# Transposes and values one step nearer to the scores, in an attention that runs into a mixture of experts

## The chip, the cores and the metric

One core of a Trainium2 chip runs the whole program. The metric is the device time of one launch in microseconds. A core has five engines with a queue of instructions each: TensorE (PE, with its weight loads shown as PEld), VectorE (DVE), ScalarE (ACT), GpSimd (POOL) and SyncE (SP), which here issues nearly all the loads and stores.

## The reference

q, k and v have 4 batches, 8 heads, 576 positions and 64 columns a head. Half of the heads see the last 32 positions, the other half every 32nd position back; the rest is masked away.

```python
scores = np.where(masks, scale * (q @ k.T), -1e9)
attn = np.exp(scores - max); attn /= attn.sum(-1) + 1e-9
x = (attn @ v) as [2304, 512]
P = exp(x @ w_gate - max); 8 rounds of row and column normalization
out = sum over 8 experts e of P[:, e:e+1] * (np.maximum(x @ w1[e], 0) @ w2[e])
```

## The kernel before

The attention is cut into 32 steps: 4 batches, 4 pairs of heads, 2 halves of the positions. A step has 4 to 6 blocks of 64 keys. Its parts are functions of their own:

- `load_qk` and `load_v` issue its loads on SP; a tile of q and k has 3 buffers, one of v has 5.
- `at_scores` (line 251) makes the scores on PE in 20 to 40 small matmuls, into both PSUM buffers of the tag "s".
- `at_masks` (270) scales, masks and finds the extremes on DVE, block by block; `at_exp` (281) takes the exponentials on ACT. For the steps in `early` ACT leaves the sums out.
- `at_normalize` makes 1e-9 plus the sum and its reciprocal on DVE (291, 292; before them the sum itself, line 290, for the steps in `early`), and POOL multiplies (293).
- `at_transpose` transposes the result on PE (303), and DVE copies it out of PSUM (307, 309).
- `at_values` multiplies by v on PE (329). `x_high` (ACT, 361) and `x_low` (DVE, 366) write the result into x as two parts, a rounded one and the rest. Every product of the experts is made of three products of such parts.

Work is put into each engine's queue in the order of the code, and an engine takes its queue in order. There are first 8 rounds (`at_k` 0 to 7, loop at line 1123), which hold almost only attention. They also split the first weight tiles of expert 0: `split_w` rounds on ACT (193) and subtracts on POOL (194). `begin_layer1` (450) puts first products of expert 0 into late rounds, and `keep_busy` (1118) matmuls that nobody reads. Then come 36 slots (line 1214). A slot holds 12 matmuls of the first layer (`layer1`), their relu (467, 468), 6 matmuls of the second layer (`layer2`, line 487), and in the first 27 slots one step's share of the attention, each part of another step. In slots 6, 7, 13, 14, 20 and 21 the gate's products and transposes stand too (378, 387). From slot 4 on POOL prepares sums and weights for the later part (565, 581, 649 to 653, 194). After the slots come the other 7 experts, in which PE's products are made by a scheme with fewer multiplications, and the attention has no part.

In a slot the order is: layer 1, `attention_values` (values of step `at_k - 3`, x, loads), `attention_scores` (scores, masks, exponentials of step `at_k`), layer 2 of the slot before, `attention_rest` (transposes of step `at_k - 2`, then the normalizing of `at_k - 1`), and POOL's work at the end. Slot s has `at_k` = 8 + s.

Of the kernel before, what the change touches and what calls it, by code (L numbers as in the profile page):

```python
# [8 lines left out]
F32 = mybir.dt.float32  # L9
# [57 lines left out]
def kernel(  # L67
# [10 lines left out]
    P = 128  # L78
# [3 lines left out]
    NP = NDT  # L82
# [19 lines left out]
    pools = {}  # L102
# [39 lines left out]
    def chunk(ci):  # L142
        n = min(CH, NT - ci * CH)
        o = 2 * NDT * CH * ci
        return reg[:, o : o + 2 * NDT * n].rearrange("p (i k t) -> p i k t", i=2, k=NDT)
# [63 lines left out]
    NS = len(steps)  # L209
    QK = -(-max(sum(_columns(*x)[:2]) + BR for x in STEPS) // P) * P  # L210
    qk_t, v_t, scored, sms, sums_t, pts, moved, mxs = ({} for _ in range(8))

    def load_qk(k):
        if k < NS:
            nq, nk, _ = _columns(*steps[k][1:])
            t = pools["qkv"].tile([P, QK], F32, tag="qk", name=f"qk_{k}", bufs=3)
            blocks = _blocks(*steps[k][1:])
            q0, ks, m = blocks[-1]
            end = nq + max(nk, ks[-1] + BR)
            nc.sync.dma_start(t[:, :end], qkv[k, :, :end])  # L220
            qk_t[k] = t

    def load_v(k):
        if k < NS:
            nq, nk, nv = _columns(*steps[k][1:])
            blocks = _blocks(*steps[k][1:])
            n, nh = len(blocks), len(blocks[0][1])
            half = -(-n // 2) * nh * 2 * DH
            tv = pools["qkv"].tile([P, 6 * 2 * DH], F32, tag="v", name=f"v_{k}", bufs=5)
            src = qkv[k, :BR, nq + nk : nq + nk + nv]  # L230
            for i, v in enumerate((src[:, :half], src[:, half:])):
                nc.sync.dma_start(tv[BR * i : BR * (i + 1), : v.shape[1]], v)
            v_t[k] = tv[:, :half].rearrange("p (n h j d) -> p n h j d", h=nh, j=2, d=DH)

    def at_scores(k):
        b, p, hf = steps[k]
        t = qk_t.pop(k)
        nq = _columns(p, hf)[0]
        blocks = _blocks(p, hf)
        n = len(blocks)  # L240
        half = -(-n // 2)
        order = [i + half * x for i in range(half) for x in range(2) if i + half * x < n]
        scs = [ps.tile([P, 3, BR], F32, tag="s", name=f"sc_{k}_{i}") for i in range(2)]
        for i in order:
            q0, ks, _ = blocks[i]
            m, par = BR // len(ks), i // half
            for j in range(2):
                sl = slice(DH * j, DH * j + DH)
                for h, k0 in enumerate(ks):
                    o = BR * (j ^ par) + m * h  # L250
                    nc.tensor.matmul(  # L251
                        scs[par][o : o + m, i % half, :], t[sl, q0 + m * h : q0 + m * h + m],
                        t[sl, nq + k0 : nq + k0 + BR], start=True, stop=True,
                    )
        scored[k] = scs, order, half

    def at_masks(k):
        b, p, hf = steps[k]
        scs, order, half = scored.pop(k)
        n = len(order)  # L260
        sums_t[k] = st_p.tile([P, 6], F32, tag="sums", name=f"sums_{k}")
        sm = pools["at"].tile([P, 6, BR], F32, tag="sm", name=f"sm_{k}")
        mx = mxs[k] = st_p.tile([P, 6], F32, tag="mx", name=f"mx_{k}")
        for c, i in enumerate(order):
            if _is_local(p):
                mask = mlocal if hf or i else mlocal0
            else:
                mask = mstrided

            nc.vector.tensor_tensor_reduce(  # L270
                out=sm[:, c, :], in0=scs[i // half][:, i % half, :], in1=mask[:, :BR],
                op0=ALU.add, op1=ALU.min, scale=-SCALE, scalar=3.0e38,
                accum_out=mx[:, c : c + 1],
            )
        sms[k] = sm, n
# [10 lines left out]
    def at_normalize(k):  # L286
        sm, n = sms[k]
        rs = sums_t.pop(k)[:, :n]
        if k in early:
            nc.vector.tensor_reduce(rs, sm[:, :n, :], axis=AX.X, op=ALU.add)  # L290
        nc.vector.tensor_scalar_add(rs, rs, 1e-9)
        nc.vector.reciprocal(rs, rs)
        nc.gpsimd.tensor_tensor(
            sm[:, :n, :], sm[:, :n, :], rs.unsqueeze(2).to_broadcast([P, n, BR]), op=ALU.mult
        )

    def at_transpose(k):
        sm, n = sms.pop(k)
        pt = pts[k] = pools["qkv"].tile([P, 3, P], F32, tag="pt", name=f"pt_{k}", bufs=3)
        tp = ps.tile([P, 3, P], F32, tag="t", name=f"tp_{k}")  # L300
        for c in range(0, n, 2):
            m = min(2, n - c)
            nc.tensor.transpose(  # L303
                tp[: m * BR, c // 2, :],
                sm[:, c : c + m, :].rearrange("p n k -> p (n k)"), ident,
            )
        nc.vector.tensor_copy(pt[:, : n // 2, :], tp[:, : n // 2, :])
        if n % 2:
            nc.vector.tensor_copy(pt[:BR, n // 2, :], tp[:BR, n // 2, :])
# [49 lines left out]
    def x_high(k):  # L359
        for src, (hi, _) in moved[k]:  # L360
            nc.scalar.activation(hi, src, AF.Copy)

    def x_low(k):
        b = steps[k][0]
        for src, (hi, lo) in moved.pop(k):
            nc.vector.tensor_tensor(lo, src, hi.bitcast(F32), op=ALU.subtract)
        p, hf = steps[k][1:]
        if hf:
            done.extend(
                (c, p) for c in range(NC) if b * S < min(NT, (c + 1) * CH) <= (b + 1) * S  # L370
            )
# [167 lines left out]
    for p in range(NPASS):  # L539
        for k in range(NK):  # L540
            k = (k - KEEP * p) % NK
# [523 lines left out]
            next(w2n, None)  # L1065


    LAG = 3
    at_k = 0

    def attention_scores():
        if at_k < NS:
            at_scores(at_k)
            at_masks(at_k)
            at_exp(at_k)

    def attention_rest():


        nonlocal at_k  # L1080
        if 0 <= at_k - 2 < NS:
            at_transpose(at_k - 2)
        if 0 <= at_k - 1 < NS:
            at_normalize(at_k - 1)
        at_k += 1

    def attention_values():
        if at_k > WARM + 2:
            store_x(1)
        if at_k > WARM + 1:  # L1090
            at_values(at_k - LAG, "tt")
            x_high(at_k - LAG)
            x_low(at_k - LAG)
        load_qk(at_k + 2)
        load_v(at_k)

    WARM = 2 * NP - 1
    nc.scalar.dma_start(cst[:, 2:], consts[:, 2:])
    nc.scalar.dma_start(cst[:, 0], consts[:, 0])
    for k in range(3):  # L1100
        load_qk(k)
    load_v(0)
    for i in range(2):
        nc.sync.dma_start(cst[BR * i : BR * (i + 1), 1], consts[:BR, 1])
    spare = chunk(NC - 1)[:, 0, :, :].rearrange("p k t -> p (k t)")[:, : 5 * P]
    nc.gpsimd.memset(spare.bitcast(F32), 1.0)
    nc.gpsimd.memset(ones, 1.0)
    nc.gpsimd.memset(wgs.bitcast(F32), 0.0)
    for o in (QT, 3 * QT):
        nc.gpsimd.tensor_copy(cst[o : o + QT, 3, :BR], cst[o : o + QT, 2, :BR])  # L1110
    ahead = {5: [(0, (0, 1))], 6: [(1, (0, 1))], 7: [(0, (2,)), (1, (2,))]}
    early = {4: 0, 5: 1, 6: 2, 7: 3}
    late = {0: 4, 1: 5, 2: 6, 3: 7}

    def keep_busy(n, tag="l1"):
        unread = ps.tile([P, 4 * P], F32, tag=tag, name=f"unread_{at_k}_{n}")
        for _ in range(n):
            nc.tensor.matmul(unread, spare[:, :P], spare[:, P:], start=True, stop=True)  # L1118

    FILL = (1, 0, 1, 1, 0, 0, 1)  # L1120
    keep_busy(6)
    at_scores(0)
    for at_k in range(WARM + 1):
        last = at_k == WARM
        if at_k == 0:
            load_v(1)
        if at_k < WARM:
            load_qk(at_k + 3)
        if at_k not in (0, 2):
            load_v(max(2, at_k))  # L1130
        if at_k not in (0, 3):
            load_w()
        if at_k >= 3:
            x_high(at_k - 3)
        at_masks(at_k)
        if at_k:
            at_normalize(at_k - 1)
        if at_k >= 3:
            x_low(at_k - 3)
        if at_k >= 2:  # L1140
            at_transpose(at_k - 2)
        if at_k < 2:
            keep_busy(1)
        if at_k < WARM:
            at_scores(at_k + 1)
        at_exp(at_k)
        if last:
            begin_layer1(0, (0, 2 * P), *ahead[at_k][0])
        if at_k >= 2:
            at_values(at_k - 2, "yy")  # L1150
        for x in ahead.get(at_k, ())[last:]:
            begin_layer1(0, (0, 2 * P), *x)
        if at_k and FILL[at_k - 1]:
            keep_busy(FILL[at_k - 1], "l1" if at_k < 3 else "t")
        if last:
            x_high(at_k - 2)
            x_low(at_k - 2)
        if at_k in early:
            split_w(*plain[early[at_k]])
    at_k = WARM + 1  # L1160
# [231 lines left out]
```

## Time and profile before

| | us |
|---|---|
| median of 3 runs | 1535.34 (1533.87 to 1536.08) |
| the profiled execution | 1534.33 |
| its span from the first to the last instruction | 1532.5 |
| PE busy | 1521.8 |
| DVE busy | 1302.3 |
| POOL busy | 1041.0 |
| ACT busy | 546.3 |

The profiled execution lies 1.0 us below the median; 1.8 us of it lie outside the span. A busy PE is one with a matmul under way, whatever it waits for inside.

### The profile page before, as it was taken

The page shows a single profiled execution, that of the slowest core. Times are in us where ns is not written, and L with a number is a line of the kernel's source. Part 1 is how long each engine was busy: PE and PEld are TensorE (multiplying, and loading weights), DVE is VectorE, ACT ScalarE, POOL GpSimd, SP SyncE. Part 2 cuts the span into 40 slices and gives each one's busy share as a digit, 9 for nine tenths or more (in the row PEclk, how much of TensorE's full clock was granted, in tenths as well). Part 3 has the DMA queues.
Part 4 walks back from the last instruction along what each step waited for, and adds up shares of the span by engine and source line. Part 5 has one row for each costly group of instructions (what it writes and reads, how often), then busy time and mean ns, then how long its engine had stood idle before and what let it go on. Part 6 is the DMA issues. An engine that isn't in the chain of part 4 may idle for free.

```text
span 1532.5 us, 27898 instructions
## 1 busy us (share of the span) xinstructions
PE 1521.8 (99%) x10096; PEld 1445.4 (94%) x10096; DVE 1302.3 (85%) x2610; ACT 546.3 (36%) x1340; POOL 1041.0 (68%) x1056
## 2 busy tenths in 40 slices
PE   8999999999999999999999999999999999999999
PEld 6888989899999999899999999999999999999998
DVE  6665899999999999768888888888688888888888
ACT  7675344334343434242332322322323232232221
POOL 4567155555666565078888889888687787777874
PEclk9999999999999999999999999999999999999999
DMA  9778888988888888887877867767576676666662
GB/s 275 246 237 274 319 321 309 344 309 336 312 329 319 325 329 295 331 305 264 318 259 277 311 237 296 294 247 286 212 306 262 261 283 239 268 264 239 277 246 91
DMA packets 145625, 431.11 MB, mean 281 GB/s; under 512 B 35696, under 2 KB 89168, under 8 KB 130512
## 3 DMA queue, kind: packets, MB, share of 16 engines
q1 hardware_dynamic: 145200, 429.14, 75.4%
q8 instruction: 80, 1.31, 0.3%
q14 instruction: 57, 0.47, 0.1%
q10 hardware_dynamic: 288, 0.20, 0.0%
HBM read 284.54 MB, written 144.75 MB: 280 GB/s over the span
## 4 chain that ended last, share of the span: by engine, by line
PE 98%; DMA 1%; DVE 1%; ACT 0%; POOL 0%; issue 0%; SPq 0%; POOLq 0%; ACTq 0%
PE p L882 27%; PE bb L731 18%; PE yg L763 18%; PE bc L731 12%; PE ba L731 12%; PE y L487 3%; PE ph L450 3%; PE pv L329 1%; PE sc L251 1%; PE tp L303 1%; PE pl L378 1%; PE tr L912 0%; DMA qk<-in_qkv 0%; PE unread L1118 0%; ACT sm L281 0%
## 5 line engine op out<-in xcount | busy, mean ns | idle before, releaser
L890 DVE TENSOR_TENSOR total<-p,total 128x384 f32<-128x384 f32 x770 | 401.0, 556 | 0.8 <-PE p L882 0.8
L731 PE MATMUL bb<-reg 128*128 128x384 f32 x1620 | 325.9, 335 | 0.0
L731 PEld LDWEIGHTS bb<-reg 128*128 128x128 f32 x1620 | 284.9, 188 | 2.9 <-DVE u L805 0.3
L731 PE MATMUL bc<-reg 128*128 128x384 f32 x1080 | 216.2, 334 | 0.0
L731 PE MATMUL ba<-reg 128*128 128x384 f32 x1080 | 216.2, 334 | 0.0
L863 ACT ACTIVATE a<-u 128x384 fp32r<-128x384 f32 x114 | 59.9, 526 | 384.5 <-DVE u L857 382.8
L805 DVE TENSOR_TENSOR u<-bb,m 128x384 f32<-128x384 f32 x180 | 99.9, 555 | 111.4 <-PE bb L731 108.9
L731 PEld LDWEIGHTS bc<-reg 128*128 128x128 f32 x1080 | 190.1, 188 | 0.0
L731 PEld LDWEIGHTS ba<-reg 128*128 128x128 f32 x1080 | 189.8, 188 | 0.0
L939 POOL TENSOR_TENSOR s1t<-m,u 128x384 f32<-128x384 f32 x57 | 57.9, 1016 | 163.3 <-DVE m L857 163.3
L770 DVE SCALAR_TENSOR_TENSOR acc<-yg,gate,acc 128x512 f32<-128x512 f32 x197 | 139.1, 740 | 9.0 <-PE yg L763 9.0
L763 PE MATMUL yg<-w2t,h 128*128 128x512 f32 x540 | 125.5, 390 | 0.0
L763 PE MATMUL yg<-w2b,h 128*128 128x512 f32 x540 | 125.4, 390 | 0.0
L882 PE MATMUL p<-s,w2b 128*128 128x384 f32 x696 | 125.3, 334 | 0.0
L882 PEld LDWEIGHTS p<-s,w2b 128*128 128x128 f32 x696 | 121.1, 188 | 0.0
L882 PE MATMUL p<-s,w2t 128*128 128x384 f32 x672 | 121.0, 334 | 0.0
L763 PEld LDWEIGHTS yg<-w2t,h 128*128 128x128 f32 x540 | 101.1, 188 | 20.5
L763 PEld LDWEIGHTS yg<-w2b,h 128*128 128x128 f32 x540 | 101.1, 188 | 20.5
L882 PEld LDWEIGHTS p<-s,w2t 128*128 128x128 f32 x672 | 116.9, 188 | 0.0
L867 POOL TENSOR_TENSOR a<-u,a 128x384 fp32r<-128x384 f32 x114 | 116.6, 1023 | 0.0
L194 POOL TENSOR_TENSOR reg<-ra,reg 128x512 fp32r<-128x512 f32 x28 | 45.9, 1640 | 88.6 <-ACT reg L193 88.6
L805 DVE TENSOR_TENSOR u<-bc,u 128x384 f32<-128x384 f32 x180 | 99.4, 552 | 4.9 <-PE bc L731 1.8
(154 smaller groups left out, 2807.5 us busy)
## 6 DMA issues: line engine op xcount, KB each, us to landing
reg<-wd SPq DMA_DIRECT2D x56, 1792.0 KB
wd<-reg SPq DMA_DIRECT2D x30, 1792.0 KB
w2b<-w2d SPq DMA_DIRECT2D x27, 1792.0 KB
w2t<-w2d SPq DMA_DIRECT2D x26, 1792.0 KB
w2d<-w2b SPq DMA_DIRECT2D x15, 2048.0 KB
w2d<-w2t SPq DMA_DIRECT2D x15, 2048.0 KB
raws<-in_w SPq DMA_DIRECT2D x68, 256.0 KB
reg<-sd SPq DMA_DIRECT2D x12, 768.0 KB
```

The source lines that it names most:

```text
L194: nc.gpsimd.tensor_tensor(lo, src, hi.bitcast(F32), op=ALU.subtract)
L450: nc.tensor.matmul(ph[:, :n], w[:, i, dt, :], xv(x, dt, c0, n), start=(first and len(taken) == 1 and i + x == 0), stop=(len(taken) == NDT ...
L487: nc.tensor.matmul(y, h[:, a, i * P : (i + 1) * P], w[:, b, :], start=(ft == 0 and first), stop=(ft == FH - 1 and a == 1),)
L731: nc.tensor.matmul(out[:, :TN], w[:, i, k, :], xops[x][:, xi, k, :], start=(start and n == 0), stop=(n == 5), skip_group_check=True,)
L763: nc.tensor.matmul(y, hg[g, i // 3, f][:, a, o : o + P], w[:, b, f, :], start=(f == 0 and a + b == 0), stop=(f == 1 and a == 1),)
L770: nc.vector.scalar_tensor_tensor(acc[:, i, :], y, gate[:, t, e : e + 1], acc[:, i, :], op0=ALU.mult, op1=ALU.add)
L805: nc.vector.tensor_tensor(o, bank[:, :TN], s, op=ALU.add)
L863: nc.scalar.activation(t[:, 0], src, AF.Copy)
L867: nc.gpsimd.tensor_tensor(t[:, 1], src, t[:, 0].bitcast(F32), op=ALU.subtract)
L882: nc.tensor.matmul(y[:, :TN], w[:, b, wi, d, :], h[:, a, :], start=(a + b == 0), stop=(a == 1),)
L890: nc.vector.tensor_tensor(o, y[:, :TN], o, op=ALU.add)
L939: nc.gpsimd.tensor_tensor(s1, m1, u3, op=ALU.add)
```

## The change

One step of the attention passes through fewer rounds or slots. There are 7 rounds and not 8. In a round or slot the transposes are those of the step before the one that is masked, and the values follow one round or slot later. Normalizing moves ahead: in a round it now stands before the masks, in a slot before the scores and masks, and the transposes of the same step stand later in the same round or slot. In a round the transposes also stand ahead of the next step's scores. Slot s now has `at_k` = 7 + s, so it takes the values of step 5 + s as before, but the scores of step 7 + s and not 8 + s, the normalizing of 6 + s and not 7 + s, and as before the transposes of 6 + s. The scores of step 7 and the normalizing of step 6 stand at the end of the last round. The loads are issued in another order, with each weight tile behind the q and k of its round, v later, and one more q and k tile ahead by a fourth buffer. The unread matmuls are put into other rounds: 10 in all and not 12.

```diff
-            t = pools["qkv"].tile([P, QK], F32, tag="qk", name=f"qk_{k}", bufs=3)
+            t = pools["qkv"].tile([P, QK], F32, tag="qk", name=f"qk_{k}", bufs=4)
...
-    LAG = 3
+    LAG = 2
...
     def attention_scores():
+        if WARM + 1 < at_k <= NS:
+            at_normalize(at_k - 1)
         if at_k < NS:
-            at_scores(at_k)
+            if at_k > WARM + 1:
+                at_scores(at_k)
             at_masks(at_k)
             at_exp(at_k)
...
-        if 0 <= at_k - 2 < NS:
-            at_transpose(at_k - 2)
-        if 0 <= at_k - 1 < NS:
-            at_normalize(at_k - 1)
+        if at_k <= NS:
+            at_transpose(at_k - 1)
         at_k += 1
...
-    WARM = 2 * NP - 1
+    WARM = 2 * NP - 2
...
     for k in range(3):
         load_qk(k)
     load_v(0)
+    load_qk(3)
...
+    load_v(1)
...
-    ahead = {5: [(0, (0, 1))], 6: [(1, (0, 1))], 7: [(0, (2,)), (1, (2,))]}
-    early = {4: 0, 5: 1, 6: 2, 7: 3}
+    ahead = {4: [(0, (0, 1))], 5: [(1, (0, 1))], 6: [(0, (2,)), (1, (2,))]}
+    early = {3: 0, 4: 1, 5: 2, 6: 3}
     late = {0: 4, 1: 5, 2: 6, 3: 7}
+    v_of = {0: 2, 2: 3, 3: 4, 4: 5, 5: 6}
...
-    FILL = (1, 0, 1, 1, 0, 0, 1)
+    FILL = (1, 1, 1, 1, 0, 0, 0)
...
-        if at_k == 0:
-            load_v(1)
-        if at_k < WARM:
-            load_qk(at_k + 3)
-        if at_k not in (0, 2):
-            load_v(max(2, at_k))
-        if at_k not in (0, 3):
+        if at_k <= 4:
+            load_qk(at_k + 4)
+        if at_k in v_of:
+            load_v(v_of[at_k])
+        if at_k:
             load_w()
-        if at_k >= 3:
-            x_high(at_k - 3)
-        at_masks(at_k)
+        if at_k >= 2:
+            x_high(at_k - 2)
         if at_k:
             at_normalize(at_k - 1)
-        if at_k >= 3:
-            x_low(at_k - 3)
+        at_masks(at_k)
         if at_k >= 2:
-            at_transpose(at_k - 2)
-        if at_k < 2:
+            x_low(at_k - 2)
+        if at_k == 0:
             keep_busy(1)
-        if at_k < WARM:
+        else:
+            at_transpose(at_k - 1)
+        if not last:
             at_scores(at_k + 1)
         at_exp(at_k)
...
-        if at_k >= 2:
-            at_values(at_k - 2, "yy")
+        if at_k:
+            at_values(at_k - 1, "yy")
...
         if last:
-            x_high(at_k - 2)
-            x_low(at_k - 2)
+            at_scores(at_k + 1)
+            at_normalize(at_k)
+            x_high(at_k - 1)
+            x_low(at_k - 1)
```

## Rows read from the trace of the kernel before

**Rows 1.** The page's first line.

```profile
span 1532.5 us, 27898 instructions
```

**Rows 2.** Stretches of the span: length, each engine's busy time, granted clock, DMA share, GB/s.

```profile
0.00:25.00 25.00, 19.08 (x431) 14.28 (x431) 15.56 (x125) 17.73 (x84) 10.49 (x19) 1.00 0.85 257
...
50.00:145.00 95.00, 94.89 (x1593) 81.74 (x1595) 62.74 (x359) 64.57 (x301) 64.54 (x98) 1.00 0.80 253
```

**Rows 3.** Waits of PE from 0 to 50 us: total us, times, longest.

```profile
PE sc L251 <- DMA qk<-in_qkv: 2.1, 3, 1.3
PE pv L329 <- DVE pt L307: 2.0, 3, 1.1
PE unread L1118 <- POOL reg L1106: 1.4, 1, 1.4
PE pv L329 <- issue: 0.8, 1, 0.8
PE y L487 <- POOL w2t L194: 0.4, 2, 0.2
```

**Rows 4.** The chain that ended last, in order of time: start us, us, what.

```profile
8.97 5.38 DMA qk<-in_qkv
...
67.60 1.59 PE y L487 x6
...
92.57 0.35 PE pg L387 x4
```

**Rows 5.** Timeline of the rounds: start us, us, engine, line, names [idle before].

```profile
5.38 0.35 ACT L281 ACTIVATE sm<-sm,mx 128x64 f32<-128x64 f32 x1 [2.43 <-DVE mx L270]
...
15.00 0.61 PE L329 MATMUL pv<-pt,v 64*64 64x54 f32 x24
...
23.52 0.56 PE L329 MATMUL pv<-pt,v 64*64 64x54 f32 x20 [0.58 <-DVE pt L307]
```

**Rows 6.** Groups of instructions, slots only: count, busy us, mean ns, idle before.

```profile
L281 ACT ACTIVATE sm<-sm,mx 128x64 f32<-128x64 f32 x95 | 31.9, 337 | 15.7 <-DVE mx L270 15.7
```

**Rows 7.** Timeline of the rounds, parts of steps 3 to 6.

```profile
16.09 1.31 ACT L281 ACTIVATE sm<-sm,mx 128x64 f32<-128x64 f32 x5
...
17.28 0.64 ACT L193 ACTIVATE w<-raws 128x512 fp32r<-128x512 f32 x1
17.28 0.83 POOL L293 TENSOR_TENSOR sm<-sm,sums 128x384 f32<-128x384 f32 x1 [1.15 <-DVE sums L292]
...
18.07 1.28 POOL L194 TENSOR_TENSOR w<-raws,w 128x512 fp32r<-128x512 f32 x1
...
18.85 0.47 DVE L290 TENSOR_REDUCE sums<-sm 128x5 f32<-128x320 f32 x1
...
19.38 0.49 PE L303 MATMUL tp<-cst,sm 128*128 128x128 f32 x3
...
20.18 0.55 DVE L307 COPY pt<-tp 128x384 f32<-128x384 f32 x1
```

**Rows 8.** Timeline of slot 9 and the end of slot 8.

```profile
66.09 0.72 POOL L293 TENSOR_TENSOR sm<-sm,sums 128x320 f32<-128x320 f32 x1 [2.98 <-DVE sums L292]
...
66.33 0.89 PE L329 MATMUL pv<-pt,v 64*64 64x32 f32 x40
...
66.77 1.42 POOL L565 TENSOR_TENSOR sx<-reg 128x256 f32<-128x256 f32 x2
...
67.63 0.56 DVE L366 TENSOR_TENSOR reg<-pv,reg 128x192 fp32r<-128x192 f32 x2 [0.29 <-ACT reg L361]
...
68.10 0.21 DVE L270 CUSTOM_DVE_ANT_0 sm<-sc,cst 128x64 f32<-128x64 f32 x1
...
69.02 0.49 PE L303 MATMUL tp<-cst,sm 128*128 128x128 f32 x3
```

**Rows 9.** Timeline of slot 2: the normalizing of one step.

```profile
36.26 0.16 DVE L291 TENSOR_SCALAR sums<-sums 128x4 f32<-128x4 f32 x1
...
36.80 0.61 POOL L293 TENSOR_TENSOR sm<-sm,sums 128x256 f32<-128x256 f32 x1 [3.31 <-DMA v<-in_qkv]
```

More of the change, by code (lines that the diff above doesn't have):

```diff
@@ L1148 @@
             begin_layer1(0, (0, 2 * P), *ahead[at_k][0])
-        if at_k >= 2:
-            at_values(at_k - 2, "yy")
+        if at_k:
+            at_values(at_k - 1, "yy")
         for x in ahead.get(at_k, ())[last:]:
             begin_layer1(0, (0, 2 * P), *x)
-        if at_k and FILL[at_k - 1]:
-            keep_busy(FILL[at_k - 1], "l1" if at_k < 3 else "t")
+        if at_k and FILL[at_k]:
+            keep_busy(FILL[at_k], "l1" if at_k < 3 else "t")
         if last:
-            x_high(at_k - 2)
-            x_low(at_k - 2)
+            at_scores(at_k + 1)
+            at_normalize(at_k)
+            x_high(at_k - 1)
+            x_low(at_k - 1)
         if at_k in early:
```

## The prediction

> **What bounds the kernel now.** I read the page first: the span is 1532.5 us [rows 1], and the table gives PE 1521.8 of them, so all that can be won is some 11 us in which PE idles, and the matmuls that nobody reads. Then the stretches: from 50 to 145 us, nearly all of the slots that hold attention, PE is busy 94.89 of 95 us [rows 2]. It has nothing left to give there. In the first 25 us it is busy 19.08 [rows 2]. The list of PE's waits says what the first 50 us lose: 2.1 us on q and k, 2.0 on copies of transposes by DVE, 0.8 on nothing the profile shows, 0.4 on POOL's half of a weight tile, and 1.4 at the very start that the change doesn't touch [rows 3]. The worst load took 5.38 us [rows 4]. So at most 5.3 us, 0.35%, are there to win. What is there to lose is not in such a list: in the slots PE never waits because each step's parts lie a slot apart. The question is how much of that distance PE's full queue needs.
>
> **The loads.** Reordering costs no byte. q and k of steps 3 to 6 come with fewer bytes in front, and the fourth buffer frees their issue from older scores; v is asked for two slots ahead of use and not three. A slot is some 4.2 us (1.43 of layer 1, values, scores, 1.59 of layer 2, 0.33 of transposes), and two are above the worst 5.38 [rows 4]. SP's queue holds the same issues, those of v behind the same stores. I take the 2.1 us of waits on q and k as gone, and no new ones.
>
> **The rounds.** The new order ties engines into a ring. Normalizing step k needs all its exponentials; the masks of k+1 stand behind it on DVE; the exponentials of k+1 wait for these. From one step's exponentials to the next lie the division (0.31), the first mask and the hand-overs: 0.75. I carried this by hand. Exponentials of step 0 start at 5.38 [rows 5] and end at 6.8 (0.34 each [rows 6]). Then product (8.05), transposes (8.5), scores of step 2 (9.2), values of step 0 (9.85). ACT writes these to x (10.4) and makes step 2's six exponentials (12.4). Division, product 0.83, transposes 0.49 and copy 0.55 [rows 7] put step 2's values at 15.0 to 15.1, where they are now: 15.00 [rows 5]. The waits on q and k go, and the ring puts waits in their place.
>
> From there on weights are split too. The split stands ahead of the product on POOL: exponentials of k end, ACT rounds the tile 0.64, POOL subtracts 1.28, the product follows 0.83, transposes 0.49, copy 0.55, then DVE's next normalizing with its sum (0.47 plus 0.36), first mask 0.3, exponentials of k+2 1.31 [rows 7], with some 0.3 of hand-overs: 6.5 us for two rounds. At present masks, sums, x and copies keep DVE busy for 2.6 a round and nothing else holds it. Values come at 18.2, 21.85 and 24.5; the last of these stands at 23.52 now [rows 5]. Layer 1 of slot 0 needs them in x; it ends at 26.5, against 25.6. By then either order has made the scores of steps 0 to 7. The rounds cost 0.9 us.
>
> **Slots 0 and 1.** Step 7 was masked in the rounds and now is in slot 0, behind layer 1's relu on DVE: masks from 27.4, exponentials to 29.35. Slot 0's split follows on ACT (30.0) and POOL (31.3), and only behind it comes the product of step 7, which slot 1's transposes now need in the same slot: 32.05. PE has ended that slot's layer 2 at 30.6. It waits 1.5 us, and the copy of slot 0 adds 0.2: 1.7. In slots 3 and 4 the 0.4 us on POOL's weight half [rows 3] goes, since the product no longer stands late ahead of it. The 0.8 us without a cause I leave as they are; they may go too.
>
> **Slots 2 to 25.** Here the order of the code decides. Normalizing stands behind `x_low` of the values of the same slot, and the transposes that need it stand behind layer 2 of the same slot. So two paths run from the end of the values. On PE: scores and layer 2. On the others: x on ACT and DVE, division, product. In slot 9 values end at 67.22 (66.33 + 0.89), PE comes to the transposes at 69.02, so it needs 1.80. DVE is through with x at 68.10 [rows 8]. From the start of the addition to that of the product is 0.54 (36.26 to 36.80 [rows 9]), the product of five blocks takes 0.72 [rows 8], the hand-over 0.05: 69.41, or 2.19 after the values. PE waits 0.39. The same subtraction in every slot, with 0.75 to 1.05 from values to the end of x (four blocks to six), products of 0.61, 0.72 and 0.83 [rows 7 to 9], and the scores that now stand in the slot:
>
> slot 2 0.31, 4 0.11, 5 0.56, 9 0.39, 10 0.29, 11 0.13, 12 0.39, 14 0.16, 15 0.35, 17 0.50, 18 0.40, 19 0.14, 21 0.13, 22 0.60, 23 0.30, 25 0.86. The sum is 5.6 us. Eight slots pay nothing, most because the gate's products (0.35 in slot 14 [rows 4], more elsewhere) or longer scores lengthen PE's path. The stalls add, since each slot's path starts anew at its values. Where POOL's 3.3 to 3.9 us of preparation fill a slot, the product also waits for POOL; for slots 9 to 12 and 17 to 22 I add 0.4. Bounds: nothing, if x ends earlier by a better ACT queue; or 1 us more in each of slots 23 and 24, where x ended up to 1 us late behind DVE's other waits.
>
> The page of the Trainium skill on trace analysis (Perfetto Trace Analysis, GPSIMD part of "Per-engine timelines") says that spans of GpSimd are unreliable and that starts should be subtracted. Here it agrees in kind: the product of 0.72 at 66.09 is followed by the next operation at 66.77, 0.68 later [rows 8]. By that each of the 16 stalls is 0.04 shorter and the sum 0.6 us less.
>
> **The sum.** 1534.3 (the profiled execution) + 0.9 + 1.7 - 0.4 + 5.6 + 0.4 = 1542.5 us. That execution lies 1.0 below the median, so against the median it could read 1543.5; I keep 1542.5. Low end of this case 1538, with half the stalls hidden; high end 1547, with the late x of slots 23 and 24, POOL's backlog and 1 us more in the rounds.
>
> **Rivals.**
>
> *The slots hide it* (chance 0.17). x, division and product fit beside layer 2, say because ACT and DVE reach x sooner. For it: in eight slots PE's path is the longer one already. Against it: slot 9's row, where x starts at once and is still too late. Only rounds and slots 0 to 4 count: 1534.3 + 0.9 + 1.7 - 0.4 = 1536.5, no change by what can be measured (about 0.2%, 3.1 us).
>
> *Faster* (0.10). The waits in the rounds on q and k and on copies go (2.1 + 2.0 [rows 3]), 0.4 in slots 3 and 4 as well, and the ring is no longer than DVE's 2.6 a round: 1534.3 - 4.5 = 1529.8. It decides if step 2's values come before about 13 us; then the first layer starts earlier and every wait shown is won. Against it: exponentials, division and masks of successive steps can no longer overlap. If only the loads' 2.1 are won, it is 1532.2, no change.
>
> *The clock* (0.06). The granted clock is 1.00 in all stretches [rows 2], that is 2.4 GHz, though PE waits up to 1.3 us at a time [rows 3]. My rounds have three gaps of 1.2 to 1.8 us between 6 and 17 us, with less work between. If the clock falls to 1.2 GHz there and stays low for the rounds, PE's some 13 us of work from 6 to 25 us double, and the gaps hide about half: 1542.5 + 7 = 1549. TensorE: Matmul & The Clock Gate ("The HAM clock gate" in the Trainium skill) has such a rule: an idle array is throttled to half its clock. Nothing in this trace shows it fall.
>
> The main case has 0.67. Faster by over 0.2%: 0.10; within: 0.17; slower: 0.73. The range takes in the main case and most of the "hidden" one: 1534.5 to 1547, with a tenth below and less than a tenth above.
>
> **What would show it.** Right: PE waits on POOL's product (line 293) at the transposes, in some 16 slots, 0.1 to 0.9 us each; PE busy 50 to 145 us falls to about 94%; a wait of over 1 us at slot 1's transposes; no wait on q and k; values of step 2 near 15 us, those of step 5 at 24 to 25 us. Wrong: no PE waits in the slots, so the path from values to product is shorter than I read, or the values of step 5 before 23 us. A clock below 1.00 in the rounds would make it worse than the range.

## The result and the profile after

The changed kernel takes 1546.19 us (median of 6 runs, 1545.47 to 1547.3) against 1535.37 before (6 runs, 1533.87 to 1536.18). The ratio is 1.0073, interval 1.006 to 1.0086: slower by 10.8 us. The profiled execution of the changed kernel takes 1545.99 us.

The page's first line, after:

```profile
span 1544.2 us, 27884 instructions
```

The stretches, after (length, each engine's busy time, granted clock, DMA share, GB/s), which answer to [rows 2]:

```profile
0.00:25.00 25.00, 21.14 (x359) 15.46 (x359) 14.08 (x98) 14.34 (x65) 9.25 (x18) 1.00 0.90 255
25.00:50.00 25.00, 22.15 (x409) 17.60 (x408) 14.51 (x97) 16.69 (x79) 11.54 (x13) 1.00 0.83 254
50.00:145.00 95.00, 91.10 (x1508) 75.64 (x1506) 59.13 (x360) 62.87 (x299) 61.16 (x97) 1.00 0.73 223
```

PE lacks 3.9 us of 95 in a stretch in which it lacked 0.1. Its waits from 0 to 50 us, and the last line from 50 to 145 us (total us, times, longest), which answer to [rows 3]:

```profile
PE tp L303 <- POOL sm L293: 4.3, 6, 1.6
PE unread L1122 <- POOL reg L1109: 1.4, 1, 1.4
PE pv L329 <- DVE pt L307: 0.5, 2, 0.4
...
PE tp L303 <- POOL sm L293: 3.6, 8, 0.6
```

The waits on q and k are gone. In their place the transposes wait for POOL's product of line 293, in the rounds and in the slots. The timeline after shows this in three places: a round (19 to 21 us), slot 1 (32 to 35 us) and slot 9 (71 to 74 us, which answers to [rows 8]):

```profile
19.31 0.53 DVE L290 TENSOR_REDUCE sums<-sm 128x6 f32<-128x384 f32 x1
...
19.51 1.27 POOL L194 TENSOR_TENSOR w<-raws,w 128x512 fp32r<-128x512 f32 x1 [1.73 <-ACT w L193]
19.88 0.92 DVE L291 TENSOR_SCALAR sums<-sums 128x6 f32<-128x6 f32 x1
20.12 1.65 PE L450 MATMUL ph<-reg,w 128*128 128x256 f32 x6
...
20.84 0.19 DVE L292 RECIPROCAL sums<-sums 128x6 f32<-128x6 f32 x1
...
21.20 0.83 POOL L293 TENSOR_TENSOR sm<-sm,sums 128x384 f32<-128x384 f32 x1 [0.42 <-DVE mx L270]
...
26.66 0.56 PE L329 MATMUL pv<-pt,v 64*64 64x54 f32 x20 [0.16 <-DVE pt L307]
...
32.40 1.28 POOL L194 TENSOR_TENSOR w<-raws,w 128x512 fp32r<-128x512 f32 x1 [2.65 <-ACT w L193]
...
32.97 0.61 DVE L366 TENSOR_TENSOR reg<-pv,reg 128x192 fp32r<-128x192 f32 x3
...
33.75 0.19 DVE L292 RECIPROCAL sums<-sums 128x5 f32<-128x5 f32 x1
...
34.10 0.72 POOL L293 TENSOR_TENSOR sm<-sm,sums 128x320 f32<-128x320 f32 x1 [0.42 <-DVE mx L270]
...
34.88 0.55 PE L303 MATMUL tp<-cst,sm 128*128 128x128 f32 x3 [1.64 <-POOL sm L293]
...
71.06 0.89 PE L329 MATMUL pv<-pt,v 64*64 64x32 f32 x40
...
72.36 0.56 DVE L366 TENSOR_TENSOR reg<-pv,reg 128x192 fp32r<-128x192 f32 x2 [0.24 <-ACT reg L361]
...
72.83 0.16 DVE L291 TENSOR_SCALAR sums<-sums 128x5 f32<-128x5 f32 x1
...
73.39 0.72 POOL L293 TENSOR_TENSOR sm<-sm,sums 128x320 f32<-128x320 f32 x1 [1.00 <-DVE mx L270]
...
74.17 0.55 PE L303 MATMUL tp<-cst,sm 128*128 128x128 f32 x3 [0.25 <-POOL sm L293]
```

Read slot 9 from below: the transposes start when the product ends (73.39 + 0.72 = 74.11), the product follows the division, and the division starts when DVE is through with x. From the end of the values (71.95) to the transposes are 2.22 us; before they were 1.80 [rows 8]. In slot 1 the subtraction of a weight split ends at 33.68 and the product starts at 34.10: it does not wait for the subtraction but for the division, which stands behind x (its last part ends at 33.58) as in slot 9. In the round there is something that I had not looked for: the addition of 1e-9 to six sums takes 0.92 us on DVE, where the one in slot 9 takes 0.16.

The end of the values of some steps shows where the 11.7 us between the two spans come in:

| values of step | end before | end after | later by |
|---|---|---|---|
| 3 | 18.64 | 20.19 | 1.6 |
| 5 (last of the rounds) | 24.09 | 27.23 | 3.1 |
| 7 (slot 2) | 33.66 | 37.68 | 4.0 |
| 14 (slot 9) | 67.22 | 71.95 | 4.7 |
| 22 (slot 17) | 104.28 | 111.81 | 7.5 |
| 31 (last) | 145.58 | 157.08 | 11.5 |

After that nothing more is lost.

### The profile page after: what moved, and what is told of

Read it like the earlier page. It is cut to its first block, busy times and chain, and to the rows that moved or that the text cites. A ratio compares the mean times of both kernels' runs of the same rounds, so it can differ in the third digit from the quotient of the medians.

```text
span 1544.2 us, 27884 instructions
## 1 busy us (share of the span) xinstructions
PE 1529.4 (99%) x10094; PEld 1448.0 (94%) x10094; DVE 1302.7 (84%) x2610; ACT 546.3 (35%) x1340; POOL 1042.6 (68%) x1056
## 4 chain that ended last, share of the span: by engine, by line
PE 94%; DVE 2%; ACT 1%; POOL 1%; issue 0%; POOLq 0%; ACTq 0%; DVEq 0%
PE p L882 26%; PE bb L731 18%; PE yg L763 17%; PE bc L731 12%; PE ba L731 12%; PE ph L450 3%; PE y L487 2%; PE tp L303 1%; PE pv L329 1%; POOL sm L293 1%; ACT sm L281 1%; DVE reg L366 1%; PE sc L251 1%; PE pl L378 1%; DVE total L890 0%
```

## The experiments

The first four versions ask which part of the change costs; the next four, why; the last four, whether it can be got back. Each ratio is to the kernel before on the same chip, whose median was 1535.02 us beside e1 to e4, 1534.45 beside e5 to e8 and 1534.12 beside e9 to e12.

**e1: the slots alone.** The eight rounds and the loads of before, with the slots of after; the first of these slots takes over step 7, which the rounds still begin.

```diff
-    LAG = 3
+    LAG = 2
...
-        if at_k < NS:
+        if WARM < at_k <= NS:
+            at_normalize(at_k - 1)
+        if WARM < at_k < NS:
             at_scores(at_k)
...
-        if 0 <= at_k - 2 < NS:
-            at_transpose(at_k - 2)
-        if 0 <= at_k - 1 < NS:
-            at_normalize(at_k - 1)
+        if at_k <= NS:
+            at_transpose(at_k - 1)
...
-    at_k = WARM + 1
+    at_k = WARM
```

> The 8 rounds and their loads of the kernel before, with the slots of the changed one (division and product of a step ahead of its transposes in the same slot). Theory A (in the slots the product comes behind the x of the same slot and PE waits for it): the changed kernel lost 7.3 us from the values of step 9 (4.2 us late) to those of step 31 (11.5 us late), so about 1542.5 here, 7 us above before, with the same waits of PE on POOL's product. Rival R1 (the loss is that of the rounds, the loads and the fourth buffer; the slots only pass it on): 1535 to 1536.

1542.98 us (1542.03 to 1545.54), ratio 1.0055 [1.0039, 1.007]. A held. PE is busy 91.05 us from 50 to 145, as after, and has the same line of waits there (on the product, 3.6 us in 8 waits). The slots cost most of it without the new rounds.

**e2: division first in the slot.** The change whole, but the normalizing of a slot stands ahead of layer 1 and so ahead of relu and x on DVE; the step, its data and its slot are the same.

```diff
     for slot, (u, c, ft) in enumerate(slots):
         busy = at_k < NS + LAG
+        if WARM + 1 < at_k <= NS:
+            at_normalize(at_k - 1)
...
     def attention_scores():
-        if WARM + 1 < at_k <= NS:
-            at_normalize(at_k - 1)
```

> The changed kernel with the normalizing of a slot's step moved ahead of layer 1 of that slot, so that it no longer stands behind the x of that slot's values on DVE. Theory A: the waits of PE at the transposes go from slot 2 on, some 6.5 us: 1539.7. Rival R2 (POOL's own preparation or the exponentials are what the transposes wait for, so the place of the division doesn't matter): 1546.

1539.18 us (1538.63 to 1539.69), ratio 1.0029 [1.0018, 1.0041]: 6.8 us back by the two ratios. A held. The stretch from 50 to 145 us is full again:

```profile
50.00:145.00 95.00, 95.00 (x1634) 81.50 (x1632) 62.70 (x378) 66.62 (x319) 62.09 (x99) 1.00 0.76 239
```

**e3: the loads alone.** Before, with the order of the loads and the fourth buffer of after.

```diff
-    ..., tag="qk", name=f"qk_{k}", bufs=3)
+    ..., tag="qk", name=f"qk_{k}", bufs=4)
...
+        if at_k <= 5:
+            load_qk(at_k + 4)
+        if at_k in v_of:
+            load_v(v_of[at_k])
+        if 1 <= at_k <= 6:
+            load_w()
```

> The kernel before with the new order of the loads in the rounds and the fourth q and k buffer alone. Theory B (the 2.1 us in which PE waits for q and k in the rounds are on the path): 1533.3, 2 us below before. Rival R3 (DVE's chain of masks, sums, x and copies is just behind, and takes over): 1535, no change.

1535.32 us (1533.93 to 1538.09), ratio 1.0005 [0.9996, 1.0014]: no change. B fell, and the time is the one that R3 named. Its waits from 0 to 50 us:

```profile
PE sc L251 <- DVE mx L270: 2.1, 3, 1.6
```

The scores waited 2.1 us for q and k [rows 3]; they now wait as long for the masks of an earlier step, which must give their PSUM tile free. The largest of these waits, 1.59 us, is of the edit's own making. From e3's timeline:

```profile
9.28 0.23 DVE L270 CUSTOM_DVE_ANT_0 sm<-sc,cst 128x64 f32<-128x64 f32 x1 [1.96 <-DMA cst<-in_consts]
...
10.19 0.65 PE L251 MATMUL sc<-qk 64*64 64x64 f32 x20 [1.59 <-DVE mx L270]
```

The masks of step 2 wait for constants, which SP now issues behind step 3's q and k (at 4.37 us and not 3.37); before, the same masks started at 7.69. So e3 does not show that DVE's chain, which R3 held to be just behind, would have taken over by itself. What the loads alone are worth stays open.

**e4: more unread matmuls.** After, with four unread matmuls ahead of round 1's transposes, to hold the clock.

```diff
         else:
+            if at_k == 1:
+                keep_busy(4)
             at_transpose(at_k - 1)
```

> The changed kernel with 4 unread matmuls more on PE in round 1, ahead of the transposes for which PE waits 1.5 us there. In the trace of the changed kernel the six matmuls of 256 columns at 20.1 us take 1.65 us and those at 21 us of the kernel before 0.98, so PE ran at half its clock up to some 24 us. Theory C (the clock stays low for want of dense work, and this is most of the 3 us by which the rounds end late): the matmuls of 256 columns in the rounds take 0.98 again and the time is about 1544, 2 us less. Rival R4 (the ring of exponentials, division and masks alone sets the rounds): no gain, 1546.

1545.79 us (1545.26 to 1547.19), ratio 1.0072 [1.006, 1.0085]: nothing gained. In its trace the clock is full from 6.5 to 13.3 us and half from there to 23.6, so the edit did not hold it through the rounds; C is not refuted by this run; e8 tries it again.

**e5: the rounds alone.** The rounds and loads of after, the slots of before; step 7 is masked at the end of the last round, since the old slots expect it.

```diff
-    LAG = 2
+    LAG = 3
...
+        if last:
+            at_masks(at_k + 1)
+            at_exp(at_k + 1)
-    at_k = WARM + 1
+    at_k = WARM + 2
```

> The 7 rounds of the changed kernel with their loads and fourth buffer, with step 7 masked at their end, and behind them the slots of the kernel before. In the changed kernel the values of step 5 end at 27.23 us and at 24.09 before. Theory B2 (the rounds cost these 3 us by themselves, and PE's full slots give none of it back): 1538. Rival R5 (what the rounds lose is made up in slots 0 to 4, where PE had idled 1.2 us, or is the slots' doing): 1535 to 1536.5.

1539.15 us (1538.34 to 1540.7), ratio 1.003 [1.0019, 1.0042]: 4.7 us slower than before, more than the 0.9 of my sum. The values of step 5 end at 26.35, and the lateness stays at 3.8 us from slot 3 to the end. e1 (8.0) and e5 (4.7) together cost 12.7 us where the whole change costs 10.8; the intervals of the two (6.0 to 10.7 and 2.9 to 6.4 us) leave room for that, and I did not follow it up.

**e6: masks first in the rounds.** e2, with the masks of a round ahead of its division.

```diff
+        at_masks(at_k)
         if at_k:
             at_normalize(at_k - 1)
-        at_masks(at_k)
```

> As e2_divide_first (1539.2), and in the rounds the masks of a step again stand ahead of the division of the step before, as in the kernel before; the transposes stay where the change put them. Theory D (the ring of exponentials, division, masks, exponentials sets the rounds): the exponentials of neighbouring steps overlap again, and 1 to 2 us come back: 1537.5. Rival R6 (the products on POOL behind the weight splits, and PE at half its clock, set the rounds; the place of the masks doesn't matter): 1539.

1543.42 us (1543.04 to 1544.49), ratio 1.006 [1.0046, 1.0073]: 4 to 5 us worse than e2. D fell, and so did R6, which expected no difference. Step 3's product shows it: in e2 it starts at 16.94, just ahead of the round's exponentials (17.06); in e6 the exponentials go first (17.90), and the product starts at 19.00. TensorE's scores and transposes stand behind it. PE's waits from 0 to 50 us:

```profile
PE tp L303 <- POOL sm L293: 6.6, 7, 1.8
```

**e7: old rounds, division first.** e1 with the edit of e2.

```diff
     def attention_scores():
-        if WARM < at_k <= NS:
-            at_normalize(at_k - 1)
...
         busy = at_k < NS + LAG
+        if WARM < at_k <= NS:
+            at_normalize(at_k - 1)
```

> As e1_slots_only (1543.0), with the division moved ahead of layer 1 of its slot as in e2_divide_first. Theory A (the place of the division is all that the new slots cost): 1535, the time of the kernel before, or 0.4 less for the two waits on a weight tile in slots 3 and 4. Rival R7 (scores and loads that are one slot nearer to their use cost too): 1537 or more.

1535.01 us (1533.65 to 1536.28), ratio 1.0001 [0.9992, 1.001]. A held: within the interval, the place of the division is all that the new slots cost. With it first, one slot less of distance costs nothing that the time shows, and brings nothing. One wait on the product is left in the trace, 0.9 us in slot 25, where POOL subtracts a weight first.

**e8: the clock held up.** e2, with 16 unread matmuls ahead of the transposes of rounds 1, 3, 4 and 5.

```diff
         else:
+            n = {1: 5, 3: 5, 4: 4, 5: 2}.get(at_k, 0)
+            if n:
+                keep_busy(n, "l1" if at_k < 3 else "t")
             at_transpose(at_k - 1)
```

> As e2_divide_first (1539.2), with 16 unread matmuls more, in rounds 1, 3, 4 and 5 ahead of the transposes for which PE waits there. Theory C (PE's clock falls to half for want of dense work in the rounds, and this is what they lose): the granted clock stays at 1.00 in the first 25 us and the time is 1537. Rival R8 (the clock has little part in it): 1539, or up to 1542 when the 16 matmuls, 0.2 to 0.4 us each, only stand in PE's way.

1539.34 us (1537.32 to 1541.14), ratio 1.0028 [1.0017, 1.004], as e2. Here the edit did its work: in e8 the clock is full from 10.8 us on, in e2 half from 9.35 to 26.4. Yet step 5's values start at the same time. The first line is e8's timeline:

```profile
27.15 0.56 PE L329 MATMUL pv<-pt,v 64*64 64x54 f32 x20 [0.17 <-DVE pt L307]
```

and this is e2's:

```profile
27.16 0.56 PE L329 MATMUL pv<-pt,v 64*64 64x54 f32 x20 [0.17 <-DVE pt L307]
```

The gain that C forecast did not come, and the time is R8's. But the equal end hides two things. The five unread matmuls of round 1 put step 0's transposes back. PE's lines in e8:

```profile
6.50 2.50 PE L1120 MATMUL unread<-reg 128*128 128x512 f32 x5
8.80 0.63 PE L303 MATMUL tp<-cst,sm 128*128 128x128 f32 x2
...
10.05 0.95 PE L329 MATMUL pv<-pt,v 64*64 64x32 f32 x32
```

and in e2:

```profile
8.06 0.44 PE L303 MATMUL tp<-cst,sm 128*128 128x128 f32 x2 [1.72 <-POOL sm L293]
...
9.02 0.85 PE L329 MATMUL pv<-pt,v 64*64 64x32 f32 x32
```

From step 0's values to step 5's e8 then takes 17.10 us and e2 18.14. So up to 1.0 us of the rounds may be the clock's, and this edit spent as much; a version that holds the clock without standing in PE's way was not run. At full clock, too, PE waits for the ring through DVE, POOL and ACT: 3.3 us on the product from 0 to 50 us, in e8 as in e2.

**e9: the subtraction behind the product.** e2, with GpSimd's half of each weight split of the rounds put behind the product of the next round. e10 to e12 each add one thing to the version before them.

```diff
         nc.scalar.activation(hi, src, AF.Copy)
-        nc.gpsimd.tensor_tensor(lo, src, hi.bitcast(F32), op=ALU.subtract)
+        if hold:
+            held.append((lo, src, hi))
...
         if at_k:
             at_normalize(at_k - 1)
+            split_held()
         at_masks(at_k)
```

> The version with the division first in the slot (1539.2), and in the rounds GpSimd's subtraction of the weight split stands behind the next product instead of ahead of it; ScalarE's copy of the weights stays where it was. Theory A (the addition is held up): in that version VectorE's addition to the sums takes 0.94, 0.91 and 0.41 us in three rounds (at 15.70, 19.76 and 23.87) where it takes 0.17 elsewhere, and each ends within 0.05 us of the end of a subtraction of 1.27 us on GpSimd. It is on the ring of the rounds, so with the subtraction elsewhere all three take 0.17, the values of step 5 end 1.2 to 1.75 us sooner than 27.7, and the time is 1537.7. Rival R9: the addition is not what the round waits for (the masks, the exponentials or the copies of the transposes are), so the additions shorten but step 5's values stay near 27.5 and the time near 1539. Rival R10: the weight tile that the second layer waits for comes later and takes back what was gained (a wait of y on a weight tile of over 0.5 us).

1537.11 us (1536.35 to 1537.38), ratio 1.0018 [1.001, 1.0027]. A held. The lines of e9's timeline below answer to those at 19.31 to 21.20 of after; the addition takes 0.17 us, and the subtraction follows the product:

```profile
18.92 0.53 DVE L300 TENSOR_REDUCE sums<-sm 128x6 f32<-128x384 f32 x1
19.48 0.17 DVE L301 TENSOR_SCALAR sums<-sums 128x6 f32<-128x6 f32 x1
...
20.05 0.83 POOL L303 TENSOR_TENSOR sm<-sm,sums 128x384 f32<-128x384 f32 x1 [1.44 <-DVE mx L280]
...
20.84 1.28 POOL L204 TENSOR_TENSOR w<-raws,w 128x512 fp32r<-128x512 f32 x1
```

Step 5's values end at 25.75 and not at 27.72, 1.97 sooner, and step 31's at 148.29 and not 150.38, 2.09 sooner. The intervals of the two ratios overlap (1.0018 to 1.0041 against 1.001 to 1.0027, some 1.7 us between the ratios), so the size rests on the traces. Not all of it need be the addition's: the clock is full from 21.36 us in e9 and from 26.41 in e2, and the transposes of steps 4 and 5 take 0.59 and 0.55 us where they took 0.90 and 0.74.

**e10: division ahead of the copy.** e9, with the division of step k ahead of DVE's copy of the transposes of step k-1.

```diff
         at_exp(at_k)
+        at_normalize(at_k)
+        split_held()
+        if at_k:
+            at_copy(at_k - 1)
```

> As the run before, and in each round VectorE divides step k ahead of copying the transposes of step k-1 (the subtraction of the split again behind the product). Theory A (the ring): in the version with the division first in the slot the sums of a round stood ready at 14.3, 18.8, 22.4 and 26.35 us but were reduced only at 15.2, 19.2, 23.4 and 27.2, behind the copy of the step before, which waits for TensorE's transposes and so for the product before. Taking the copy off that path gives back 0.9 + 0.4 + 1.0 + 0.85 = 3.1 us at most, of which the copies and values, put back by a division of 0.85 us each, keep some: values of step 5 end at 24.5 to 25.5 and the time is 1535.5 to 1536.5. Rival R11: the values wait for the copy in every round, so that what the division gains the copy loses: no sooner than the run before (about 1537.7).

1543.03 us (1542.87 to 1544.0), ratio 1.0058 [1.0045, 1.007]: 5.9 us worse than e9. A fell, and more is lost than R11 allowed. The timeline of one round shows the link that I had left out:

```profile
17.50 0.52 DVE L327 COPY pt<-tp 128x384 f32<-128x384 f32 x1
...
17.94 0.22 DVE L280 CUSTOM_DVE_ANT_0 sm<-sc,cst 128x64 f32<-128x64 f32 x1
...
18.07 1.00 PE L349 MATMUL pv<-pt,v 64*64 64x54 f32 x24 [0.78 <-DVE pt L327]
...
19.01 0.63 ACT L381 ACTIVATE reg<-pv 128x144 fp32r<-128x144 f32 x4 [1.85 <-PE pv L349]
...
19.50 1.54 ACT L291 ACTIVATE sm<-sm,mx 128x64 f32<-128x64 f32 x6
```

The later copy makes the values later; ACT's writing of the values to x stands ahead of the next exponentials in ACT's queue and waits 1.85 us for them, and the exponentials wait behind it though the first mask was made by 18.16, over a microsecond before. So the ring now runs through copy, values, x and exponentials: 4.2 to 4.3 us a round (values of steps 1, 2 and 3 at 13.90, 18.07 and 22.41), where e9 took 3.1 to 3.8. A new place for x was not tried.

**e11: division at the end of the slot.** e10, with the division of e2 emitted at the end of the slot before, ahead of its weight split.

```diff
-        if WARM + 1 < at_k <= NS:
-            at_normalize(at_k - 1)
...
             attention_rest()
+            if at_k <= NS:
+                at_normalize(at_k - 1)
```

> As the run before, and the division and product of a step are emitted at the end of the slot, ahead of the late weight splits, and not at the start of the next slot. Theory A: the transposes of slot 1 wait 1.2 us for a product that stands behind a subtraction of 1.3 us in GpSimd's queue although its sums were ready; with the product first the wait goes and the time is 1.0 to 1.3 us below the run before (about 1534.5 to 1535.3, level with the kernel before). Rival R12: what stands behind the product then comes late instead, the weight tiles or the split of the hidden values, and the time is that of the run before within 0.4 us.

1543.61 us (1543.28 to 1544.36), ratio 1.0062 [1.0049, 1.0074]: nothing gained on e10. R12 held. The wait at slot 1's transposes falls from 1.13 to 0.19 us, and a wait on the weight tile, whose subtraction now stands behind the product, comes in its place. From e11's waits of 0 to 50 us:

```profile
PE y L507 <- POOL w2t L199: 0.6, 1, 0.6
```

**e12: no addition.** e11, without the addition of 1e-9 to the sums.

```diff
-        nc.vector.tensor_scalar_add(rs, rs, 1e-9)
         nc.vector.reciprocal(rs, rs)
```

> As the run before, with the addition of 1e-9 to the sums left out (the sums are at least 1, so the quotients are the same numbers). Theory A: the addition of 0.17 us and the gap of 0.03 behind it are on the ring of the rounds five or six times, so it gives back 0.7 to 1.2 us. Rival R13: by now the rounds wait for something else (the exponentials' chain or the data), and the time is that of the run before within 0.4 us.

1541.13 us (1540.85 to 1541.42), ratio 1.0044 [1.003, 1.0058]: 2.5 us below e11, twice what A expected. Step 1's values end 0.4 us sooner than e11's and step 6's 1.0 sooner, as A has it; step 31's 1.9 sooner. Where the part after the rounds comes from was not looked into.

No version beats the kernel before: e7 is level with it, and e9, the best with seven rounds, is 3.0 us behind. In e9's trace 1.15 us of these are the wait in slot 1, and 1.2 come in slot 25, where the product stands behind a weight subtraction of 1.3 us on POOL.

## Why the prediction was right, and where its size was off

**What bounds.** PE's full queue in the slots had nothing to win and much to lose: right. The wait on line 293 came where it was told. PE is busy 95.9% of 50 to 145 us, where I forecast about 94%, and the list shows 8 waits there, fewer than I counted. Yet the time lost is larger than either says: a listed wait begins at the modelled end of the matmul before it. In slot 9 it is 0.25 us, and the transposes, 1.80 us behind the values before, are 2.22 behind them now: 0.42.

**Loads.** I took the 2.1 us as gone with the ring's waits in their place. They are gone. How much they were worth is not shown: with the loads of before, e1's profile has 1.6 us of them and e7's 0.5, and e3, without the ring, put a wait of its own in their place.

**Rounds, 0.9: mis-sized.** Step 5's values start at 26.66, not 24.5, in the profile. The term left out is the hold-up of the addition beside the weight subtraction. The rows that I took for the division were those of a slot where POOL was idle ahead of the product [rows 9]. In after three additions take 0.52, 0.92 and 0.42 us, 1.35 more than three of 0.17; e9 takes the meeting away and gets 2.0 back in the values, of which up to 0.5 may be the clock's. The trace of before had such a row, at the division of step 6, which I passed over:

```profile
21.02 1.28 POOL L194 TENSOR_TENSOR w<-raws,w 128x512 fp32r<-128x512 f32 x1 [0.38 <-ACT w L193]
...
21.88 0.46 DVE L291 TENSOR_SCALAR sums<-sums 128x5 f32<-128x5 f32 x1
```

Another part is in the base: three other versions with the old rounds (e1, e3, e7) end step 5's values at 25.59 to 26.25 in their profiles, where the profile that I worked from had 24.09. That profile was the one in which the clock was full from 5.44 us on, and it lay 1.0 below the median, as the prediction said; how much of the difference is the clock's is not separated. The sum has a small slip as well: 6.5 us for two rounds puts step 4's values at 21.6 at most, and not 21.85.

**Slots 0 and 1, 1.7.** The wait came where it was put, 1.64 us against 1.5, but partly by another path. I had the product behind the weight subtraction; in the trace it comes 0.42 us after that has ended, since the division stands behind x in this slot too, as in slots 2 to 25. With the division first (e2) the product does follow the subtraction, and the wait is 1.20. From step 5 to step 7 only 0.9 are lost, since waits of before fell away there, the 0.8 without a cause [rows 3] likely among them (argued, not tested).

**Slots 2 to 25, 5.6 + 0.4 - 0.4: right in mechanism, short by 1.9.** From step 7 to step 31 the lateness grows by 7.5. The chain from the values to the transposes, worked out in each slot as in slot 9, was within 0.05 us in most: 2.36, 2.19, 2.08 and 1.95 in slots 5, 9, 10 and 11 (measured 2.38, 2.22, 2.10 and 1.96). It was longer where x came late: 2.53 for 2.17 in slot 12, 0.2 more in slots 17 and 22. In slot 15 it was 2.75 for 2.36, and there it is the addition again, held until a subtraction on POOL ends:

```profile
102.13 1.30 POOL L194 TENSOR_TENSOR reg<-raws,reg 128x512 fp32r<-128x512 f32 x1
...
102.89 0.56 DVE L291 TENSOR_SCALAR sums<-sums 128x5 f32<-128x5 f32 x1
```

I had named late x and POOL's preparation and given them 0.4; the hold-up was in no term. e2 and e7 confirm the reason: with the division ahead of x, 7 to 8 us come back.

**The sum.** 1542.5 is 3.7 short of 1546.2. By the points above: 1.0 for the profile below the median, some 2 for the addition, 1.9 for the slots, less 0.8 in slots 0 and 1 make about 4.

**Rivals.** "The slots hide it" fell (e1), "faster" fell: step 2's values came at 15.87, not before 13. The clock rival named a thing that did happen: in after the trace has no record of the clock before 23.85 us, and until then the durations are those of 1.2 GHz (the six matmuls at 20.12 take 1.65 us; the same six took 0.98 before). Its price of 7 us did not come: the whole miss is 3.7 us, and e8, at 2.4 GHz from 10.8 us on, is at most 1.0 us faster than e2 from step 0's values to step 5's.

The page of the Trainium skill that I drew on (Perfetto Trace Analysis, GPSIMD part of "Per-engine timelines") is borne out in kind only: slot 9's product ends at 74.11 by its span and the next operation on POOL begins at 74.07. It is worth 0.04 us a stall, and the transposes start by the longer of the two.

## What to carry to other kernels

When a step is brought one slot nearer to its user, keep its place in every queue that it passes as early as its data allow: the same division cost some 7 us behind two operations of the same slot and nothing that the time shows ahead of them. Before pricing a ring, write down each engine's queue and what stands ahead in it, since a move that frees one engine (e6, e10) lengthened the ring through another. When a wait goes from a list, another can take its place, one that the edit itself made (the constants behind q and k in e3, the weight tile in e11), so try the edit alone and read what waits there now before the gain is counted.

## What the runs showed of the hardware

An addition of 1e-9 to 128 x 6 numbers takes 0.17 us on DVE by itself and 0.92 us when POOL's subtraction is under way: it then ends with it (20.80 against 20.78 in after; in e2 at 16.64, 20.67 and 24.28 against 16.61, 20.65 and 24.26; in before at 22.34 against 22.30). The reduction before it is not lengthened (0.53 beside the subtraction, 0.53 in e9). The Trainium skill states this (SBUF — State Buffer, "Who interferes with whom"): VectorE and GpSimd share a pair of ports that the first to come holds for its whole instruction, operations like an addition of a constant can need it, and reductions never do. The traces agree, and with that page the row at 21.88 us of before could have put the cost into the sum beforehand.

PE at 1.2 GHz is not the same as PE idle. In after it was busy 21.14 of the first 25 us, largely with matmuls of 64 x 64 and transposes, and stayed at the lower level until 23.85 us; e8, with more unread matmuls of 128 x 512 in the rounds, has the higher from 10.8 us. The column of the granted clock reads 1.00 for after's first stretch because its first record begins at 23.85 us: a duration of a known matmul is the better witness.
